# Moving the second weight block's preparation from the first tick to the sixth

## The chip, the cores and the metric

The kernel is one program on one core of a Trainium2 chip. The core has five instruction streams that run side by side and meet through semaphores: TensorE (PE, with its weight loads shown as PEld), VectorE (DVE), ScalarE (ACT), GpSimd (POOL) and SyncE (SP). SP, ACT and POOL also issue DMAs; the profile names their issuing side SPq, ACTq and POOLq. The metric is the device time of one execution in microseconds (us), lower being better.

## The reference

The inputs are float64. Attention over 8 batches, 8 heads, 576 positions and 64 columns a head is followed by a gated feed-forward layer with 512 columns in and 1536 in the middle:

```python
scores = scale * np.matmul(q, k.transpose(0, 1, 3, 2))
s_pos = np.maximum(s, 0.0)
cum = np.cumsum(s_pos, axis=-1)
bias = -(cum[:, :, :, None] - cum[:, :, None, :])
scores = np.where(causal, -1000000000.0, scores + np.minimum(bias, 0.0))
attn = softmax(scores)                       # max, exp, sum, division by hand
x = np.matmul(attn, v)                       # heads side by side: 4608 x 512
gate = 1.0 / (1.0 + np.exp(-(x @ w_gate)))
out = (gate * (x @ w_val)) @ w_out
```

The bias of a row of scores is a constant of the row plus the running sum of its column, so a head needs one row of 576 numbers, which is copied to all 128 partitions.

## The kernel before

**Ticks.** The main loop (L900) runs over ticks `n`. A head has five tiles of rows (`TILES`, `NTL` = 5), so tick `n` belongs to head `i = n // 5`, and the first head is ticks 0 to 4. Its work is spread over several ticks: scores at tick `n`, subtraction of the minimum and the exponential one tick later, turning and the product with v after that. The first eight heads (`NN` = 8) are computed in float32 by functions whose names begin with `n_`; the later ones with operands split into 16-bit pairs. The feed-forward layer starts at tick 44 (`NE`) and runs beside the attention from then on.

**One early head.** `n_prep` turns q and k on PE (L614) and copies them out of PSUM on ACT (L618, L619, L621). `n_s` multiplies them (L631). `n_max` adds the bias row and finds the row's minimum on DVE (L643, with a short read of the accumulator), and then ACT takes the exponential (L644). `n_turn` transposes the exponentials on PE (L653) and copies them out on ACT (L654). `n_av` multiplies with v (L662). The tiles of a head come from the widest, t = 4 (576 columns), to the narrowest, t = 0 (64 columns); the exponential of (0, 0) is the last of the first head and is traced in tick 5.

**The bias rows.** The running sums of all heads are made at the start on DVE (L162 to L166) and stored to DRAM (L167). Each head after the first loads its row back on SP (`load_crow`, L447), and POOL copies it to all partitions (`spread_crow`, L451). DVE's L643 of that head needs it.

**The weight blocks.** The weights are 18 blocks: 12 of w_gate and w_val, 6 of w_out. `load_weight(n)` issues the two DMAs of a block, 512 KB each: on SP for blocks 0 and 1 (L284, before the loop), on ACT for the others (L286, and L279 for w_out). `weight_step` (L365) takes the next block: it first issues the loads whose room has come free, then `decode_weight` turns the pairs of 32-bit words of a float64 into float32 (L298 on ACT, L299 to L301 on DVE), and `split_weight` finds a scale for the block (eight matmuls L310, then DVE L313, L332, L334) and splits it in two 16-bit parts (L337 on ACT, L338 on DVE). Three rooms serve the first 12 blocks in turn (`room`): block 3 takes block 0's, block 4 takes block 1's. So the step of block 1 issues the loads of blocks 2 and 3, and the step of block 2 that of block 4. In the profile the first room is `ws` (decoded into `wa`), the two others lie in `w2all`.

**When steps come.** Before tick 44 the loop traces steps by L1044, up to `min(2 + n // 8, 6)`: blocks 0 and 1 in tick 0, block 2 in tick 8, block 3 in tick 16. The squares of v (L186, fed by POOL's loads L184) come in ticks 1 to 4.

**What sets the order.** A planner that simulates the program orders each engine's instructions (L1125): of those that it takes to be ready it picks by priority, which follows the order of tracing, except that the first heads' work is raised by `first()`. Each engine then runs its list strictly in that order. Two tools bend it: `keep_in_program_order` puts an instruction behind the one traced just before it on its engine (the loads of block 2 have it, L288), and `issue_after(x)` puts all that is traced inside it on the engine of `x` behind `x`; both are about the order of issue and add no wait for an end.

Of the kernel before, what the change touches and what calls it, by code (L numbers as in the profile page):

```python
# [14 lines left out]
AF = mybir.ActivationFunctionType  # L15
# [10 lines left out]
def tile_attention_then_gated_ffn(  # L26
# [11 lines left out]
    nc = tc.nc  # L38
# [11 lines left out]
    NTL = len(TILES)  # L50
# [32 lines left out]
    def halves(x):  # L83
        return x.rearrange("p (a n) -> p a n", a=2)
# [11 lines left out]
    e_t, pf_t = {}, {}  # L96
# [156 lines left out]
    def room(n):  # L253

        o, f = wsteps[n]
        if o == 0:
            return raw[f % 3], dec[f % 3], n - 3
        i, j, last = outroom[f // 2]
        return raw[i], dec[j], last

    def load_weight(n):
        o, f = wsteps[n]
        fs = slice(f * P, (f + 1) * P)
        r, d, _ = room(n)
        for x, src in enumerate((w_out,) if o else (w_gate, w_val)):
            src = src[f * P : (f + 2) * P, :] if o else src[:, fs]
            if wide:
                src = src.bitcast(I32)
                dst = r.rearrange("p n t -> p (n t)")
            else:  # L270
                dst = d.bitcast(F32)
            if o == 0:
                src = src.rearrange("(c p) n -> p c n", p=P)
                dst = dst.rearrange("p (c x n) -> p c x n", c=NC, x=2)[:, :, x]
            else:

                src = src.rearrange("(x p) (h n) -> x p h n", p=P, h=8)
                dst = dst.rearrange("p (h x n) -> x p h n", x=2, h=8)
                ins = nc.scalar.dma_start(dst[0], src[0])  # L279
                if n < NF + 2:  # L280
                    tc.keep_in_program_order(ins)
                src, dst = src[1], dst[1]
            if n < 2:
                nc.sync.dma_start(dst, src)  # L284
            else:
                ins = nc.scalar.dma_start(dst, src)  # L286
                if n == 2 or NF <= n < NF + 2:
                    tc.keep_in_program_order(ins)  # L288

    def decode_weight(n):  # L290

        o, f = wsteps[n]
        r, a, _ = room(n)
        if not wide:
            return a.bitcast(F32), None
        m = w2all[:, f // 2].rearrange("p l h x n -> p (l h x n)") if o else w1[f].rearrange("p c g l n -> p (c g l n)")
        m = m.bitcast(I32)
        nc.scalar.activation(a.bitcast(F32), r[:, :, 1].bitcast(F32), AF.Copy, scale=2.0 ** -112)  # L298
        nc.vector.tensor_scalar(m, a, 3, 0x7FFFFFF8, ALU.logical_shift_left, ALU.bitwise_and)  # L299
        nc.vector.scalar_tensor_tensor(a, a, -0x80000000, m, ALU.bitwise_and, ALU.bitwise_or)  # L300
        nc.vector.scalar_tensor_tensor(a, r[:, :, 0], 29, a, ALU.logical_shift_right, ALU.bitwise_or)  # L301
        return a.bitcast(F32), m
# [60 lines left out]
    wnext = {"load": 0, "step": 0, "tick": 0}  # L363

    def weight_step():  # L365
        n = wnext["step"]
        while n and wnext["load"] < len(wsteps) and room(wnext["load"])[2] < n:
            if not NF <= wnext["load"] < NF + 2:
                load_weight(wnext["load"])
            wnext["load"] += 1  # L370
        split_weight(n, *decode_weight(n))
        wnext["step"] = n + 1
# [213 lines left out]
                                    x16.rearrange("p l n -> p (l n)"))  # L586


    qT, kT, nA = {}, {}, {}

    def n_load(p):
        b, h0 = divmod(2 * p, H)
# [42 lines left out]
    def n_max(i, t):  # L635
        q0, m, w = TILES[t]
        acc = wp.tile([P, 1], F32, tag="em", name=f"em{i}_{t}", bufs=3)[:m]
        ps, r, e = scores_of(i, t), rl[i][:m, :w], e_t[t][:m, :w]
        if w > 512:
            ps, r, e = ps[:m, :, : w // 2], halves(r), halves(e)  # L640
        else:
            ps = ps[:m, :w]
        nc.vector.tensor_tensor_reduce(e, ps, r, 1.0, MASKED, ALU.add, ALU.min, acc)  # L643
        nc.scalar.activation(e_t[t][:m, :w], e_t[t][:m, :w], AF.Exp, bias=acc, scale=-1.0)  # L644

    def n_turn(i, t):

# [245 lines left out]
    NE, NOFF = 44, 87  # L893
# [6 lines left out]
    for n in range(nticks + 12):  # L900
        if n == NTL * EARLY:
            more_room()
        i, t = divmod(n, NTL)
# [41 lines left out]
        if i < NH:  # L945
            p, j = divmod(i, 2)
            b, h = divmod(i, H)
            if t == 0 and i + 1 < NH:
                load_crow(i + 1)
            if t == (2 if i >= NN else 0) and i + 1 < NH:  # L950
                spread_crow(i + 1)
            if i + 2 < NN:
                if j == 0 and t == 1:
                    n_load(p + 1)
                    load_v(p + 1)
                if j == 1 and t == 2:
                    with first():
                        n_prep(p + 1)
            elif j == 0 and i + 2 < NH:
                if t == (2 if spare else 1 if i >= NN else 0) and p + 1 not in qk32:  # L960
                    load_qk(p + 1)
                if t == 2 and i < NN:
                    load_v(p + 1)
            if NN <= i and i + 1 < NH and j == 1 and t == 2:
                load_v(p + 1)
            if NN <= i and j == 0 and t == 0:
                split_v(p)
            if not spare:
                late = i >= NN
                if i + 2 >= NN and j == 0:  # L970
                    if t == 2 + late:
                        qk_square(p + 1)
                    if t == 3 + late:
                        qk_scale(p + 1)
                if n == NTL * (NN - 1) - 1 or NN <= i and t == 0:
                    split_qk(max(i + 1, NN))
                if n == NTL * (NN - 1) + 1 or NN <= i and t == 2:
                    swap_k(i + 1)
            elif i <= EARLY + 1:
                if j == 0:  # L980
                    if t == 1:
                        split_qk(i + 1)
                    if t == 3:
                        swap_k(i + 1)
                        load_qk(p + 2)
                else:
                    if t == 0:
                        qk_square(p + 1)
                    if t == 1:
                        qk_scale(p + 1)  # L990
                    if t == 2:
                        split_qk(i + 1)
                    if t == 4:
                        swap_k(i + 1)
                        split_qk(i + 2)
                        load_qk(p + 3)
            elif j == 0 and i + 2 < NH:
                if t == 0:
                    if i == EARLY + 2:
                        swap_k(i + 1)  # L1000
                    qk_square(p + 1)
                if t == 1:
                    qk_scale(p + 1)
                if t == 2:
                    split_qk(i + 2)
                if t == 4:
                    swap_k(i + 2)
            elif j == 1 and i + 2 < NH:
                if t == 1:
                    split_qk(i + 2)  # L1010
                if t == 3:
                    swap_k(i + 2)
                    if i + 6 < NH:
                        load_qk(p + 3)
            if b == 0:
                if 1 <= n < 1 + vch:
                    v_square(0, n - 1)
                if n == 1 + vch:
                    v_scale(0)
            if b == 0:  # L1020
                if t == 2 and 1 <= h < 1 + vch:
                    v_square(1, h - 1)
                if t == 4 and 1 <= h < 1 + vch:
                    v_square_sum(1, h - 1)
                if t == 1 and h == 6:
                    v_scale(1)
            elif b == 1:
                if VSQ <= n < VSQ + vch:
                    v_square(2, n - VSQ)
                if VSQ + 5 <= n < VSQ + 5 + vch:  # L1030
                    c = VSQ + 4 + vch - n
                    v_square_sum(2, c)
                if n == VSQ + 11:
                    v_scale(2)
            elif b + 1 < B:
                if t == 0 and 2 <= h < 2 + vch:
                    v_square(b + 1, h - 2)
                if t == 4 and 2 <= h < 2 + vch:
                    v_square_sum(b + 1, h - 2)
                if t == 4 and h == 2 + vch:  # L1040
                    v_scale(b + 1)
            if n in OUT:
                load_weight(NF + OUT.index(n))
            while n < NE and wnext["step"] < min(2 + n // 8, 6):  # L1044
                weight_step()

        if n >= NE and state["u"] < 2 * NF:
            fdone = min(NF, int((n - NE + 1) * FPT))
# [19 lines left out]
        m = n - (11 if n > 2 * NTL * H + 30 else 7)  # L1068
# [60 lines left out]
```

## Time and profile before

| what | value |
|---|---|
| median of 3 runs | 1143.78 us |
| lowest and highest run | 1140.69, 1146.30 us |
| the profiled execution, its own time | 1143.07 us |
| its span, first to last instruction | 1141.3 us |
| mean granted TensorE clock | 0.99 |
| PE busy | 1091.1 us, 96% of the span |
| DVE busy | 829.2 us, 73% |
| ACT busy | 753.0 us, 66% |
| POOL busy | 201.2 us, 18% |
| read from and written to HBM, mean | 58 GB/s over the span |

The shares are means over stages with different limits: what a change in the first 30 us is worth has to be read from those 30 us and from whether what follows can keep a gain. A row of the timeline gives start, duration, engine, line, operation, tiles, and in brackets how long the engine stood idle before it and what ended that. A row of the chain of waits gives start, duration and what the end of the program was waiting for at that time. A row of the table by stretches gives, for each engine, its busy time and count, then the granted TensorE clock, the share of the DMA engines and GB/s.

### The profile page before, as it was taken

The numbers are of one execution on the slowest core, as the hardware profiler recorded it, in microseconds if no ns is written. First come the engines' busy times: TensorE is split into PE (matmuls) and PEld (weight loads), VectorE is DVE, ScalarE is ACT, GpSimd is POOL, SyncE is SP. The second block draws the span as 40 slices with busy tenths as digits, with TensorE's granted clock in tenths as the row PEclk, the third lists the DMA queues.
The fourth block names the chain that finished last, engine by engine and source line by source line (L and its number), as shares of the span: only waits on it lengthen the run. The fifth ranks groups of instructions, "written<-read, shape, count | busy, mean of one in ns | idle before, by whom it ended". The sixth has DMA issues, their size and how long they took to land.

```text
span 1141.3 us, 30312 instructions
## 1 busy us (share of the span) xinstructions
PE 1091.1 (96%) x11796; PEld 854.8 (75%) x11796; DVE 829.2 (73%) x2357; ACT 753.0 (66%) x1474; POOL 201.2 (18%) x471
## 2 busy tenths in 40 slices
PE   6897878899999999999999999999999999999998
PEld 4776766757787787788777777778877887787775
DVE  6758989876787777766565577777777779682854
ACT  5868667767786777676656577768776666343533
POOL 3302101022232222221111112212121212000000
PEclk9999889999999999999999999999999999999999
DMA  9776896997989798775736469787977664200000
GB/s 270 215 206 140 180 165 144 183 186 163 174 176 173 158 177 162 155 152 116 169 66 149 103 152 164 150 166 156 179 134 164 145 117 93 41 20 2 20 1 37
DMA packets 445357, 157.62 MB, mean 138 GB/s; under 512 B 403551, under 2 KB 435295, under 8 KB 445214
## 3 DMA queue, kind: packets, MB, share of 16 engines
q1 hardware_dynamic: 418974, 128.17, 57.6%
q10 hardware_dynamic: 23040, 16.78, 5.0%
q0 software_dynamic: 3200, 10.75, 2.6%
q8 instruction: 92, 1.51, 0.5%
q14 instruction: 51, 0.42, 0.1%
HBM read 56.92 MB, written 9.58 MB: 58 GB/s over the span
## 4 chain that ended last, share of the span: by engine, by line
PE 70%; DMA 9%; DVE 8%; issue 5%; ACT 4%; SPq 2%; POOL 1%; ACTq 0%; POOLq 0%; DVEq 0%
PE gv L714 33%; PE o L745 21%; PE tv L831 3%; PE s L491 3%; PE s L489 2%; DMA v<-in_v_dram 2%; PE ta L831 1%; DVE e L529 1%; PE av L564 1%; PE av L562 1%; PE av L563 1%; PE na_ps L662 1%; DMA T<-qk 1%; DMA w2all<-in_moe_w_out_dram 1%; DMA x<-x 1%
## 5 line engine op out<-in xcount | busy, mean ns | idle before, releaser
L714 PE MATMUL gv<-x,w 128*128 128x256 f16 (+3 forms) x6336 | 553.9, 245 | 9.8 <-DVE t2f L721 8.8
L714 PEld LDWEIGHTS <-w 128*128 128x128 f16 x6336 | 480.2, 98 | 63.4 <-issue 12.0
L745 PE MATMUL o<-w2all,h 128*128 128x512 f16 x1296 | 313.9, 379 | 1.9 <-ACT h L729 1.9
L530 ACT ACTIVATE e<-e,em 128x576 f32<-128x576 f32 x280 | 153.1, 556 | 88.8 <-DVE em L529 86.0
L745 PEld LDWEIGHTS <-h 128*128 128x128 f16 x1296 | 123.4, 98 | 109.1 <-ACT h L729 2.3
L511 POOL TENSOR_SCALAR_AFFINE_SELECT rl<-rl 128x128 f32<-128x128 f32 (+1 forms) x240 | 88.4, 369 | 499.2 <-DVE em L529 456.2
L529 DVE CUSTOM_DVE_ANT_0 e<-s,rl,qkcf 128x576 f32<-128x576 f32 x280 | 151.2, 544 | 28.8 <-PE s L491 12.8
L729 ACT ACTIVATE h<-t,hsc 128x256 f16<-128x256 f32 x192 | 96.3, 503 | 92.7 <-DVE t L721 90.4
L719 ACT ACTIVATE th<-gv,scb 128x256 f32<-128x256 f32 (+3 forms) x264 | 99.0, 403 | 65.5 <-PE gv L714 53.9
L539 DVE SCALAR_TENSOR_TENSOR p<-e,p 128x384 f16<-128x384 f32 x224 | 103.2, 499 | 41.1 <-ACT p L534 40.3
L721 DVE SCALAR_TENSOR_TENSOR t<-th,gv 128x256 f32<-128x256 f32 x168 | 69.7, 415 | 63.9 <-ACT th L719 63.8
L534 ACT ACTIVATE p<-e 128x1152 f16<-128x1152 f32 x112 | 111.9, 1000 | 3.4 <-DMA pt<-p 0.9
L730 DVE SCALAR_TENSOR_TENSOR h<-t,hsc,h 128x256 f16<-128x256 f32 x192 | 93.4, 487 | 27.4 <-ACT h L729 25.0
L562 PE MATMUL av<-v,pt 128*128 128x65 f16 x560 | 67.7, 193 | 2.5 <-DMA pt<-p 2.5
L451 POOL PARTITION_BROADCAST cr<-cr x63 | 59.4, 949 | 55.9 <-ACT th L719 21.1
L489 PE MATMUL s<-T 128*128 128x288 f16 (+2 forms) x246 | 64.5, 280 | 3.8 <-DVE em L529 3.0
L563 PE MATMUL av<-v,pt 128*128 128x64 f16 x560 | 67.7, 192 | 0.0
L564 PE MATMUL av<-v,pt 128*128 128x65 f16 x560 | 67.6, 194 | 0.0
L491 PE MATMUL s<-T 128*128 128x288 f16 (+2 forms) x246 | 61.5, 277 | 4.0 <-DMA T<-T 4.0
L562 PEld LDWEIGHTS <-pt 128*128 128x128 f16 x560 | 52.5, 98 | 8.3 <-DMA pt<-p 3.4
L563 PEld LDWEIGHTS <-pt 128*128 128x128 f16 x560 | 52.5, 97 | 4.5
L564 PEld LDWEIGHTS <-pt 128*128 128x128 f16 x560 | 52.7, 97 | 0.2
(209 smaller groups left out, 1539.9 us busy)
## 6 DMA issues: line engine op xcount, KB each, us to landing
v<-v SPq DMA_DIRECT2D x56, 162.5 KB
v<-in_v_dram SPq DMA_DIRECT2D x64, 128.0 KB
out_dram<-io POOLq DMA_DIRECT2D x32, 256.0 KB, 3.4
T<-T SPq DMA_DIRECT2D x82, 72.0 KB
t2f<-in_v_dram SPq DMA_DIRECT2D x20, 288.0 KB
qk<-in_q_dram SPq DMA_DIRECT2D x17, 288.0 KB
qk<-in_k_dram SPq DMA_DIRECT2D x17, 288.0 KB
w2all<-in_moe_w_gate_dram ACTq DMA_DIRECT2D x7, 512.0 KB
```

Of the source, the lines that this page charges most:

```text
L491: nc.tensor.matmul(ps[:, : b_ - a], lhs, T[i][:, 2, a:b_], start=False, stop=not mask)
L529: nc.vector.tensor_tensor_reduce(e, ps, r, c, MASKED, ALU.add, ALU.min, acc)
L530: nc.scalar.activation(e_t[t][:, :w], e_t[t][:, :w], AF.Exp, bias=acc, scale=-1.0)
L534: nc.scalar.activation(p_s[h_][:, 0], e_s[h_], AF.Copy, scale=PSCALE)
L539: nc.vector.scalar_tensor_tensor(flat[:, LOW[t] * P : (LOW[t] + t) * P], e_t[t][:, : t * P], PSCALE, flat[:, kb * P : (kb + t) * P], ALU.m ...
L562: nc.tensor.matmul(AV[i][:, t], hi, v_[:, D : 2 * D + 1], start=kb == 0, stop=False)
L563: nc.tensor.matmul(AV[i][:, t, 0:D], hi, v_[:, 0:D], start=False, stop=False)
L564: nc.tensor.matmul(AV[i][:, t], lo, v_[:, D : 2 * D + 1], start=False, stop=False)
L714: nc.tensor.matmul(ps[:, gv, a:e], w1[f][:, cc, gv, wl], x_of(b, cc)[:, xl, c0 + a : c0 + e], start=(c == 0), stop=(c == 3 * NC - 1))
L719: nc.scalar.activation(th[:, a:e], ps[:, 0, a:e], AF.Tanh, scale=scb[b][:, f : f + 1])
L729: nc.scalar.activation(h[:, 0], t2, AF.Copy, scale=hsc[:, f : f + 1])
L745: mm = nc.tensor.matmul(ps[:m], h[:, hl, tt * P : tt * P + m], w2[f][:, wl], start=(f == 0 and c == 0), stop=(f == NF - 1 and c == 2))
```

## The change

`n_max` keeps the exponential of the first head's last tile in a list. The loop traces only one weight step in ticks 0 to 4, so the second block's step is traced in tick 5, after that exponential, and everything that this step puts on ACT (the DMA issues of blocks 2 and 3, L298 and L337) is queued behind it. The number of steps from tick 5 on is as before.

```diff
-    qT, kT, nA = {}, {}, {}
+    qT, kT, nA, e_last = {}, {}, {}, []
...
         nc.vector.tensor_tensor_reduce(e, ps, r, 1.0, MASKED, ALU.add, ALU.min, acc)
-        nc.scalar.activation(e_t[t][:m, :w], e_t[t][:m, :w], AF.Exp, bias=acc, scale=-1.0)
+        ins = nc.scalar.activation(e_t[t][:m, :w], e_t[t][:m, :w], AF.Exp, bias=acc, scale=-1.0)
+        if (i, t) == (0, 0):
+            e_last.append(ins)
...
-            while n < NE and wnext["step"] < min(2 + n // 8, 6):
-                weight_step()
+            while n < NE and wnext["step"] < min((1 if n < NTL else 2) + n // 8, 6):
+                with tc.issue_after(e_last[0].ins) if wnext["step"] == 1 else ExitStack():
+                    weight_step()
```

The loads of block 2 are also kept behind what was traced just before them on ACT: that was L337 of block 0, and is now the exponential itself.

## The prediction

> **What bounds the kernel now.** First the table by stretches, cut at 250 and 260 us, to see which stage can keep a gain.
>
> ```profile
> 0.00:260.00 260.00, 218.16 (x1951) 171.05 (x1952) 209.83 (x594) 190.12 (x355) 45.08 (x96) 0.96 0.82 188
> 250.00:1141.30 891.30, 882.89 (x9906) 688.99 (x9904) 625.33 (x1779) 569.22 (x1131) 158.10 (x380) 1.00 0.62 124
> ```
>
> The first busy time is PE's. From 250 us on it is busy 882.89 of 891.30 us, so only 8.41 us are idle: a gain that arrives there reaches the end nearly whole. In the first 260 us it is idle 41.84 us and no engine is full: there chains of waits decide, and the change lies in that part. The chain that ended last shows which:
>
> ```profile
> 8.20 7.67 DMA w2all<-in_moe_w_val_dram
> ...
> 15.89 1.12 ACT w2all L298
> 17.01 0.56 ACT e L644
> ```
>
> The end of the program hangs on the second half of block 1's load (issued at 8.20, landed at 15.87), then on ACT's decoding of that block, then on an exponential of the first head. A weight block that nothing needs yet holds up attention. The timeline shows why:
>
> ```profile
> 14.11 0.08 DVE L643 DVE_READ_ACCUMULATOR2_ANT em<- 128x1 f32 x1
> 15.66 0.08 DVE L643 DVE_READ_ACCUMULATOR2_ANT em<- 128x1 f32 x1
> 15.94 0.08 DVE L643 DVE_READ_ACCUMULATOR2_ANT em<- 128x1 f32 x1
> 15.89 1.12 ACT L298 ACTIVATE w2all<-w2all 128x1024 f32<-128x1024 f32 x1 [3.56 <-DMA w2all<-in_moe_w_val_dram]
> 16.15 0.08 DVE L313 DVE_READ_ACCUMULATOR wj<-wps 128x1 f32 x1
> 16.91 0.66 ACT L644 ACTIVATE e<-e,em 128x448 f32<-128x448 f32 x1
> 17.05 0.69 DVE L299 TENSOR_SCALAR w<-w2all 128x1024 int32<-128x1024 int32 x1 [0.82 <-ACT w2all L298]
> 17.66 0.21 DVE L643 CUSTOM_DVE_ANT_0 e<-s,cr 64x64 f32<-64x64 f32 x1
> 20.03 0.35 ACT L644 ACTIVATE e<-e,em 64x64 f32<-64x64 f32 x1
> ```
>
> The minimum of tile 3 (448 columns) was ready at 14.19, yet its exponential began at 16.91: ACT stood 3.56 us before L298. DVE likewise waited with L299 in front of the minimum of the last tile.
>
> **The change part by part.** *Head 0.* With L298 behind the last exponential, the one of tile 3 can begin at 14.19, 2.72 us earlier; tiles 2 and 1 are ready at 15.74 and 16.02. DVE is free for the last tile's minimum at 16.23, so that is done at about 16.5. With 0.56 and 0.47 us for the exponentials of tiles 2 and 1 (estimated from the 0.66 and 0.35 us of the rows beside them) and perhaps one 0.5 us copy between, the last exponential ends at 17.0 to 17.5 instead of 20.38.
>
> *Step 1 on its engines.* It adds no instruction. L298 (1.12 us) begins at 17.0 to 17.5, 1.1 to 1.6 us later than now. Whether that costs anything is seen at the end of its DVE part, where the room comes free for block 4:
>
> ```profile
> 17.86 1.21 DVE L300 SCALAR_TENSOR_TENSOR w2all<-w2all,w 128x1024 int32<-128x1024 int32 x1
> 21.34 0.29 DVE L313 TENSOR_SCALAR_CACHE_REDUCE wj<-wps 128x128 bf16<-128x128 f32 x1 [2.21 <-PE wps L310]
> 21.55 1.22 DVE L301 SCALAR_TENSOR_TENSOR w2all<-w2all 128x1024 int32<-128x1024 int32 x1
> 23.20 0.37 ACTq L286 DMA_DIRECT2D w2all<-in_moe_w_gate_dram  x1
> ```
>
> L299, L300 and L301 take 0.69 + 1.21 + 1.22 = 3.12 us, after L298 from 18.1 to 18.6: they can be over at 21.2 to 21.7, where they now end at 22.77, because DVE today lies idle 2.21 us inside the step. Block 4's load (23.20) comes no later. I put this at nothing; the cover is that idle time, and if the planner leaves it where it is, L301 ends at about 24, 1.2 us late.
>
> *The four DMA issues* of blocks 2 and 3 move too, past what ACT has queued:
>
> ```profile
> 17.62 0.44 ACTq L286 DMA_DIRECT2D ws<-in_moe_w_gate_dram  x1
> 18.68 0.39 ACTq L286 DMA_DIRECT2D ws<-in_moe_w_val_dram  x1
> 19.63 0.38 ACTq L286 DMA_DIRECT2D w2all<-in_moe_w_gate_dram  x1
> 20.12 0.45 ACTq L286 DMA_DIRECT2D w2all<-in_moe_w_val_dram  x1
> 29.36 1.13 ACT L298 ACTIVATE wa<-ws 128x1024 f32<-128x1024 f32 x1
> ```
>
> From 17.0 on, back to back (1.66 us), they begin at a mean of 17.6 to 18.1 instead of 19.0: some 1.2 us earlier, not later. Block 3 is wanted at 29.36 and ACT does not wait there, so nothing is gained by it.
>
> *Where the gain is cut.* Head 1 needs its bias row first:
>
> ```profile
> 19.00 0.84 SPq L447 DMA_DIRECT2D cr<-cum_d  x2
> 23.52 1.24 POOL L451 PARTITION_BROADCAST cr<-cr  x1 [4.07 <-DMA cr<-cum_d]
> 24.79 0.76 DVE L643 CUSTOM_DVE_ANT_0 e<-s,cr 128x576 f32<-128x576 f32 x1 [0.69 <-POOL cr L451]
> 25.47 0.08 DVE L643 DVE_READ_ACCUMULATOR2_ANT em<- 128x1 f32 x1
> 25.07 1.15 ACT L337 ACTIVATE w<-w2all,wscale 128x1024 f16<-128x1024 f32 x1
> 27.69 0.41 ACT L619 ACTIVATE nq<-nq_ps 64x288 f32<-64x288 f32 x1
> 28.12 1.33 ACT L644 ACTIVATE e<-e,em 128x576 f32<-128x576 f32 x2
> ```
>
> The row lands at about 23.5 whatever head 0 does, POOL's copy and DVE's minimum follow, and 25.55 is the earliest start of head 1's first exponential. It begins at 28.12 now, since ACT is still at head 0's leftovers, L337 of block 1 and head 2's q and k. So the gain at head 1 is at most 28.12 - 25.55 = **2.57 us**, though head 0 itself gains 2.9 to 3.4. L337 goes ahead into time in which ACT is idle today; one copy such as L619 (0.41) will probably still stand in the way. Bounds: 0 (the copies and squares fill the place) and 2.57; I take 2.57 - 0.41 = 2.16, about **2.2 us**, near the upper end, because the large item (1.15) moves and the small ones are what is left.
>
> *What is carried to 250 us.* What comes next are ACT and DVE chains whose order moves along; the loads of blocks 2 and 3 are early by then. I take all of it. Sum: 1143.07 - 2.2 = 1140.9 us for the profiled execution; that lay 0.71 us under the median of 1143.78, so on the medians' scale **1141.6 us**.
>
> **The rivals.** *The DMA engines give it back.* Between 19 and 24 us the queues stand so, in the answer on DMAs (packets, MB, share of 16 engines; q10 carries ACT's loads, q1 SP's):
>
> ```profile
> q10 hardware_dynamic: 1052, 1.05, 68.3%
> q1 hardware_dynamic: 731, 0.18, 16.2%
> ```
>
> The engines are full, and SP's bias row of 2.2 KB needs from 19.00 to 23.5. Loads that begin 1.2 us earlier take, at that share, 0.683 x 1.2 = 0.8 us of them away from SP's queue before the row has landed. Then 25.55 becomes 26.35 and the gain 2.2 - 0.8 = 1.4 us: 1142.4; if a square's load on POOL also moves ahead, none is left: 1143.8. For it: the share of the engines is over 80% for the two queues together. Against: the 1.2 us count only as far as SP's queue is not empty. [...]
>
> *More is gained than head 1.* PE idles in front of the stall and is then granted a lower clock:
>
> ```profile
> 14.00:16.00 2.00, 0.47 (x3) 0.32 (x3) 2.00 (x8) 0.11 (x1) 0.57 (x1) 1.00 1.03 214
> 16.00:18.00 2.00, 0.38 (x2) 0.38 (x3) 1.18 (x9) 2.00 (x4) 0.00 (x0) 0.74 0.91 217
> 18.00:20.00 2.00, 2.00 (x9) 1.71 (x8) 1.14 (x2) 2.00 (x6) 0.54 (x1) 0.50 0.93 196
> 32.00:34.00 2.00, 0.93 (x9) 0.69 (x8) 1.71 (x2) 2.00 (x8) 0.91 (x2) 1.00 1.01 227
> 34.00:36.00 2.00, 2.00 (x11) 1.88 (x11) 0.87 (x2) 2.00 (x4) 0.50 (x1) 0.50 0.93 238
> 36.00:38.00 2.00, 2.00 (x8) 1.11 (x7) 1.05 (x1) 0.51 (x1) 0.00 (x0) 0.64 0.85 274
> 33.42 0.44 PE L662 MATMUL na_ps<-v,p 128*128 128x65 f32 x2 [1.07 <-ACT p L654]
> ```
>
> After 14 to 18 us, with PE busy 0.85 of 4 us, the clock is 0.50. The same comes again after 32 us, and there it lies on head 2's scores: at full clock 34 to 38 would be 2 x 0.50 + 2 x 0.36 = 1.7 us shorter. If an ACT that is less behind takes away the wait of 1.07 and that drop, and head 1 gains its 2.57, the sum is 5.3; a further 1.1 us saved out of the 41.84 idle by the new plan makes 6.4: 1137.4. Against: each of them must come, and further idle time may appear as easily as go. [...]
>
> *It is slower: the planner keeps head 0 late and step 1 goes into head 1.* If copies and squares of ACT are planned ahead of the last exponential, so that it still ends at 20.38, then L298 ends at 21.5 and the 3.12 us on DVE at 24.6; block 0's L338, today at 22.76, comes after:
>
> ```profile
> 22.76 1.28 DVE L338 SCALAR_TENSOR_TENSOR w<-wa,wscale,w 128x1024 f16<-128x1024 f32 x1
> ```
>
> Then head 1's minimum waits until 24.6 + 1.28 = 25.9 instead of 24.79 (1.1 us), and block 4's room is free 1.8 us later. With both on the path: 1143.78 + 2.9 = 1146.7. It decides when L301 of block 1 ends behind 22.77; when L338 of block 1 (1.28) and block 3's decoding also fall in front of minima, 1.28 + 1.12 + 3.12 = 5.5 more, up to 1152. For it: the planner put L298 in front of exponentials before, so its picture of landings is off. Against: the tiles of the first heads are raised in priority, and the squares are not.
>
> *The change does nothing:* the exponential of tile 3 waits for another load, such as that of a square of v. That is the 1143.8 end of the first rival.
>
> **How the numbers follow.** Forecast (1140.3 to 1142.8 as its own range): 0.50. DMA engines or nothing, 1142.4 to 1143.8: 0.20. More gained, around 1137.4: 0.18. Slower, around 1146.7: 0.12. A measurement of this kernel tells 0.5% (5.7 us) from no change, so faster means under 1138.1 and slower over 1149.5. Most of the gain rival and a tail of the forecast, for a plan that differs further on, give 0.19 faster; the far part of the slower rival and the same tail 0.09; 0.72 within. The range leaves out half of each outer rival and some tail: 1135.5 to 1147.
>
> **What would show it.** Right: the chain no longer passes through block 1's load; tile 3's exponential begins by 14.5, the last ends by 17.6; L298 of block 1 comes then, L301 ends by 22; the bias row still lands at about 23.5 and head 1's first exponential begins at 25.6 to 26.1; no 0.50 clock at 18 to 20; 1.5 to 2.6 us gained at 60 us and at 250 us. Wrong: the row lands after 24.3 (DMA engines), the last exponential ends at 20 (slower), or the gain at 36 us is not the gain at 250 us: then the carrying is the wrong step.

## The result: 1.05% slower

| | before | after |
|---|---|---|
| median (4 runs each) | 1142.78 us | 1156.98 us |
| lowest and highest run | 1140.69, 1146.30 us | 1153.49, 1158.44 us |
| the profiled execution | 1143.07 us | 1158.44 us |
| its span | 1141.3 us | 1156.7 us |

The ratio is 1.0105, with a 95% interval of 1.0084 to 1.0127. The forecast was 1141.6 us, in a range from 1135.5 to 1147.

First the place that the change is about. The timeline of the changed kernel, ACT, DVE and POOL between 10 and 30 us (start, duration, engine, line, tiles; in brackets the idle time before and what ended it):

```profile
14.66 0.67 ACT L644 ACTIVATE e<-e,em 128x448 f32<-128x448 f32 x1 [1.90 <-DVE em L643]
17.45 0.70 ACT L644 ACTIVATE e<-e,em 128x192 f32<-128x192 f32 x2
18.57 1.15 ACT L337 ACTIVATE w<-wa,wscale 128x1024 f16<-128x1024 f32 x1 [0.42 <-issue]
20.37 1.17 ACT L298 ACTIVATE w2all<-w2all 128x1024 f32<-128x1024 f32 x1 [0.66 <-ACT w L337]
22.13 2.52 POOL L451 PARTITION_BROADCAST cr<-cr  x2 [4.93 <-DMA cr<-cum_d]
25.27 1.22 DVE L301 SCALAR_TENSOR_TENSOR w2all<-w2all 128x1024 int32<-128x1024 int32 x1
24.63 0.78 ACT L644 ACTIVATE e<-e,em 128x576 f32<-128x576 f32 x1 [0.17 <-DVE em L643]
```

Tile 3's exponential begins at 14.66 (before 16.91), head 0's last one ends at 18.15 (before 20.38), and head 1's first begins at 24.63 (before 28.12). So the wait that was to go is gone, and head 1 begins 3.5 us sooner in this pair of profiles (how far one order scatters is told with the second experiment).

Now the same table by stretches that the prediction opened with, for the changed kernel:

```profile
0.00:260.00 260.00, 212.84 (x1836) 168.64 (x1837) 203.25 (x573) 182.57 (x340) 46.40 (x90) 0.91 0.79 180
250.00:1156.70 906.70, 898.79 (x10033) 698.75 (x10031) 637.34 (x1813) 581.23 (x1156) 163.37 (x387) 1.00 0.61 125
```

From 250 us on PE is idle for 7.91 us (before 8.41): that part is as full as it was. The loss lies in the first 260 us, where PE does less work (212.84 us busy, before 218.16) and does it at a lower mean clock (0.91, before 0.96). Cut finer, first before, then after:

```profile
0.00:40.00 40.00, 27.92 (x173) 21.41 (x174) 27.45 (x63) 25.12 (x49) 13.32 (x39) 0.91 0.91 262
40.00:60.00 20.00, 18.11 (x149) 15.49 (x146) 15.55 (x47) 16.99 (x39) 6.09 (x11) 1.00 0.73 222
60.00:120.00 60.00, 51.29 (x403) 41.84 (x402) 44.28 (x142) 49.60 (x94) 8.54 (x14) 0.97 0.67 157
120.00:140.00 20.00, 17.02 (x211) 14.46 (x209) 20.00 (x49) 10.85 (x17) 2.98 (x4) 0.91 0.97 208
140.00:200.00 60.00, 49.00 (x520) 40.85 (x517) 54.39 (x147) 44.13 (x73) 5.11 (x7) 0.94 0.78 154
200.00:240.00 40.00, 36.26 (x380) 26.93 (x381) 34.85 (x116) 27.96 (x55) 4.51 (x13) 1.00 0.93 182
240.00:340.00 100.00, 96.14 (x1148) 71.78 (x1147) 73.95 (x224) 76.36 (x157) 25.78 (x57) 1.00 0.88 174
```
```profile
0.00:40.00 40.00, 31.09 (x210) 23.93 (x210) 29.04 (x75) 27.21 (x57) 16.29 (x44) 1.00 0.92 270
40.00:60.00 20.00, 17.18 (x100) 13.91 (x99) 13.55 (x30) 14.33 (x30) 6.23 (x5) 0.79 0.76 221
60.00:120.00 60.00, 50.21 (x390) 41.09 (x389) 42.47 (x135) 47.45 (x88) 8.02 (x14) 0.93 0.61 145
120.00:140.00 20.00, 13.03 (x107) 9.78 (x108) 18.80 (x48) 10.99 (x18) 2.42 (x2) 0.67 0.90 188
140.00:200.00 60.00, 51.72 (x582) 44.25 (x581) 50.57 (x134) 40.72 (x67) 5.23 (x8) 0.94 0.73 155
200.00:240.00 40.00, 29.62 (x288) 22.84 (x286) 32.57 (x105) 28.75 (x58) 2.85 (x6) 0.95 0.84 150
240.00:340.00 100.00, 97.07 (x1111) 71.11 (x1110) 70.47 (x201) 68.64 (x143) 22.44 (x50) 0.97 0.88 164
```

One number makes such rows comparable. The end of this kernel is a long stretch in which PE is nearly always busy (898.79 of the 906.70 us from 250 us on), so what counts is how much PE work is done when that stretch begins. A stretch of length T with PE busy for b at a mean granted clock c has **lost** T - b x c: in 40 to 60 us that is 20 - 18.11 x 1.00 = 1.9 before and 20 - 17.18 x 0.79 = 6.4 after. That PE's work goes with the granted clock is the author's estimate, from 18 products with v that took 3.94 us at 0.50 and 2.12 us at 1.00 (rows below). By stretch:

| lost PE time, us | 0-40 | 40-60 | 60-120 | 120-140 | 140-200 | 200-240 | 240-340 | sum |
|---|---|---|---|---|---|---|---|---|
| before | 14.6 | 1.9 | 10.2 | 4.5 | 13.9 | 3.7 | 3.9 | 52.7 |
| after | 8.9 | 6.4 | 13.3 | 11.3 | 11.4 | 11.9 | 5.8 | 69.0 |

The sums differ by 16.3 us, the spans by 15.4. The reader is to see two things. In the first 40 us the change gains 5.7 us, more than forecast (in these two profiles). By 60 us 4.5 of them are gone, and then 120 to 140 and 200 to 240 us lose some 7 and 8 us more, in work that the change doesn't name.

### The profile page after: what moved, and what is told of

Same layout as the page of the kernel before. It is cut to its first block, busy times and chain, and to the rows that moved or that the text cites. A ratio compares the mean times of both kernels' runs of the same rounds, so it can differ in the third digit from the quotient of the medians.

```text
span 1156.7 us, 30319 instructions
## 1 busy us (share of the span) xinstructions
PE 1101.6 (95%) x11796; PEld 862.1 (75%) x11796; DVE 831.5 (72%) x2357; ACT 754.5 (65%) x1474; POOL 206.6 (18%) x471
## 4 chain that ended last, share of the span: by engine, by line
PE 76%; DMA 7%; DVE 6%; ACT 5%; issue 3%; SPq 1%; POOL 1%; ACTq 0%; POOLq 0%; DVEq 0%
PE gv L716 38%; PE o L747 22%; PE s L489 3%; PE s L491 3%; PE tv L833 3%; DMA T<-qk 2%; PE ta L833 1%; PE av L564 1%; PE av L562 1%; PE av L563 1%; DMA v<-in_v_dram 1%; DMA pt<-p 1%; DVE e L529 1%; ACT e L644 1%; PE tu L833 1%
## 5 line engine op out<-in xcount | busy, mean ns | idle before, releaser
L732 DVE SCALAR_TENSOR_TENSOR h<-t,hsc,h 128x256 f16<-128x256 f32 x192 | 93.5, 487 | 27.3 <-ACT h L731 24.9
L451 POOL PARTITION_BROADCAST cr<-cr x63 | 63.2, 1008 | 79.9 <-DMA cr<-cum_d 79.8
L562 PE MATMUL av<-v,pt 128*128 128x65 f16 x560 | 69.1, 194 | 8.0 <-DMA pt<-p 8.0
L564 PE MATMUL av<-v,pt 128*128 128x65 f16 x560 | 69.1, 196 | 0.0
```

The lines of the kernel that those rows point to most:

```text
L562: nc.tensor.matmul(AV[i][:, t], hi, v_[:, D : 2 * D + 1], start=kb == 0, stop=False)
L564: nc.tensor.matmul(AV[i][:, t], lo, v_[:, D : 2 * D + 1], start=False, stop=False)
```

## The experiments

Two questions: why isn't the early gain carried, and where do the further 15 us come from? Four theories, by their letters in the expectations. **M** (or L): block 1 is now late, and that costs. **C**: TensorE drops to half clock (granted 0.50) in the new order. **N**: the planner's new order behind the first heads is worse. **P**: any change of the trace gives a new order, good or bad by chance.

To tell them apart the order was taken out of the planner's hands. The program is traced once for each plan, the 16401 instructions are numbered alike in both, and then each engine gets a list by edges that order issue without adding a wait (code here and below is shortened):

```diff
+    for order in lists_by_engine:
+        for x, y in zip(order, order[1:]):
+            tc.add_manual_dep(y, x.name, NoSync)
```

So one kernel can have one plan up to the first minimum of some head and the other plan behind it. All runs in one table; each ratio is to before in the same session, and the lost PE time is worked out by the formula above from the rows of the one profiled execution. Three profiles of before's order (before, e2, e3) have sums of 52.7 to 55.4 us, so differences of that size mean nothing:

| kernel | median us (runs) | ratio, 95% | 0-40 | 40-60 | 60-140 | 140-340 | sum |
|---|---|---|---|---|---|---|---|
| before | 1142.8 to 1145.6 | 1 | 14.6 | 1.9 | 14.7 | 21.5 | 52.7 |
| after | 1156.98 (4) | 1.0105, 1.0084 to 1.0127 | 8.9 | 6.4 | 24.6 | 29.1 | 69.0 |
| e1 two moved | 1145.76 (12) | 1.0019, 1.0001 to 1.0036 | 17.6 | 2.4 | 14.6 | 21.8 | 56.4 |
| e2 before's order | 1144.86 (10) | 1.0008, 0.9991 to 1.0025 | 13.6 | 3.7 | 16.1 | 22.0 | 55.4 |
| e3 before's order | 1145.23 (10) | 1.0010, 0.9995 to 1.0024 | 12.0 | 3.5 | 15.5 | 21.8 | 52.8 |
| e4 sixth tick only | 1146.78 (10) | 1.0031, 1.0011 to 1.0050 | 10.9 | 2.6 | 15.3 | 23.8 | 52.7 |
| e5 after to head 4, before | 1159.79 (4) | 1.0117, 1.0088 to 1.0146 | 9.0 | 6.9 | 22.4 | 23.8 | 62.1 |
| e6 after to head 9, before | 1148.95 (10) | 1.0028, 1.0008 to 1.0049 | 9.2 | 6.6 | 16.5 | 24.9 | 57.0 |
| e7 before to head 4, after | 1155.20 (4) | 1.0091, 1.0060 to 1.0122 | 13.1 | 1.9 | 22.4 | 26.5 | 63.8 |
| e8 before to head 9, after | 1155.17 (4) | 1.0079, 1.0048 to 1.0111 | 13.3 | 1.9 | 25.2 | 24.7 | 65.1 |
| e9 after, fillers | 1156.33 (5) | 1.0097, 1.0062 to 1.0132 | 9.8 | 2.1 | 22.7 | 26.6 | 61.2 |
| e10 after, before in 9 to 12 | 1158.20 (4) | 1.0112, 1.0089 to 1.0134 | 11.7 | 6.0 | 16.1 | 36.7 | 70.6 |
| e11 after, before in 14 to 21 | 1153.34 (9) | 1.0079, 1.0054 to 1.0104 | 10.9 | 5.5 | 22.4 | 19.2 | 58.0 |
| e12 as e6, fillers | 1147.30 (11) | 1.0016, 0.9993 to 1.0039 | 8.9 | 2.1 | 17.6 | 25.0 | 53.6 |
| e13 step in the fourth tick | 1153.11 (5) | 1.0087, 1.0056 to 1.0118 | 12.9 | 2.4 | 15.8 | 30.7 | 61.9 |
| e14 other anchor | 1148.10 (10) | 1.0026, 1.0007 to 1.0046 | 7.8 | 4.2 | 16.7 | 27.3 | 56.0 |
| e15 SP's order alone | 1166.73 (4) | 1.0190, 1.0160 to 1.0219 | 13.7 | 1.9 | 19.5 | 39.9 | 75.0 |
| e16 all but SP's | 1193.46 (4) | 1.0401, 1.0348 to 1.0454 | 12.6 | 1.9 | 26.6 | 55.0 | 96.1 |
| e17 e4 to head 12, before | 1146.12 (12) | 1.0018, 0.9997 to 1.0039 | 10.8 | 2.6 | 21.0 | 23.8 | 58.3 |
| e18 e14 to head 11, before | 1140.92 (12) | 0.9978, 0.9960 to 0.9995 | 8.7 | 6.0 | 13.9 | 22.8 | 51.3 |

(In e9 and e12 up to 2.7 us of PE's busy time are the fillers' own, so their lost time is up to that much higher. One of e16's four runs took 2895 us; nothing in the records explains it.)

**The move by itself.** Before's order is pinned; only L298 of block 1 goes behind head 0's last exponential, and L299 behind that tile's minimum:

```diff
+    for what, behind in ((l298, exps[4]), (l299, minima[4])):
+        plan.remove(what)
+        plan.insert(plan.index(behind) + 1, what)
```

> Every engine keeps the order that the planner gave it before the change; only two instructions are moved: ACT's L298 of block 1 behind the first head's last exponential, DVE's L299 of block 1 behind that tile's minimum. Nothing is planned anew. Theory N (the step moved as predicted gains; the loss comes from the new order that the planner gives to all that follows): head 1's first minimum as before (24.8 us), its first exponential 1 to 2.5 us earlier than 28.1, 1 to 3 us gained at head 2 and at the end, so 0.997 to 0.999 of before. Theory M (a late block 1 is itself what costs, through its room, its loads or the work that it pushes into head 1): slower, 1.005 or more.

Measured: 1.0019. Neither branch came: no gain, and less than half of the loss that M asks for. Head 1's first minimum came 2.2 us later than before (27.0). The timelines of ACT and DVE in this run say why:

```profile
14.05 0.67 ACT L644 ACTIVATE e<-e,em 128x448 f32<-128x448 f32 x1 [1.63 <-DVE em L643]
18.37 0.45 ACTq L286 DMA_DIRECT2D ws<-in_moe_w_gate_dram  x1
18.87 0.56 ACT L644 ACTIVATE e<-e,em 128x320 f32<-128x320 f32 x1 [2.63 <-DMA nqk<-in_q_dram]
20.89 1.09 ACT L298 ACTIVATE w2all<-w2all 128x1024 f32<-128x1024 f32 x1
24.07 1.15 ACT L337 ACTIVATE w<-wa,wscale 128x1024 f16<-128x1024 f32 x1 [2.08 <-DVE wscale L334]
25.36 1.68 DVE L338 SCALAR_TENSOR_TENSOR w<-wa,wscale,w 128x1024 f16<-128x1024 f32 x1
27.02 0.74 DVE L643 CUSTOM_DVE_ANT_0 e<-s,cr 128x576 f32<-128x576 f32 x1
```

Tile 3's exponential is early (14.05), but the issue of block 3's first load (18.37; `ws` is block 3's room) still stands in ACT's list ahead of tile 2's exponential, which waits there for 2.63 us. The bracket of that row names a load of q as what ended the wait. The stall has only changed its name. On DVE block 1's pieces and then block 0's L338 stand in front of head 1's minimum. So these two moves gain nothing; the issues of the loads, which the change moves too, stayed where they were, and the whole step moved with all else pinned was not run. For M the run is a measure: block 1's L298 is 5.0 us later than before (20.89, before 15.89), and that costs 0.2%, not 1%.

**Two more measurements of before.** These two kernels, as built, have before's order on every engine, instruction for instruction, so their expectations were not tested; they show how one order scatters.

> All that the planner before puts ahead of head 4's first minimum is given in the order of the changed kernel, all the rest in the order of before. In the changed kernel head 4 begins 0.7 us later than before. Theory N: the rest is the old order, so the time is that of before within 2 us (0.998 to 1.002). Theory M: what is late early stays late, so most of the 14 us is there (1.008 or more).

> The mirror image: up to head 4's first minimum the order of before, from there on the order of the changed kernel. Theory N: 12 to 16 us slower than before (1.010 to 1.014), without block 1 being moved at all. Theory M: the time of before (0.998 to 1.003).

Measured: 1144.86 us (ratio 1.0008, 0.9991 to 1.0025) and 1145.23 us (1.0010, 0.9995 to 1.0024). In their profiles head 2's first minimum begins at 37.0 and 36.1, where it began at 38.1 in the profile of before: 2 us of scatter for one and the same order.

The scatter reaches the reading on which the change rests. Four more runs below (e7, e8, e15, e16) have before's order up to 60 us at least. In the profiles of these six, ACT waits 1.16 to 2.08 us in front of L298 of block 1 (before: 3.56), tile 3's exponential begins 0.3 to 1.3 us behind its minimum (before: 2.72), and the chain of waits doesn't pass through block 1's load. The stall that the prediction read was the longest of seven. In the first 40 us the seven profiles of before's order lose 12.0 to 14.6 us, the seven of the changed kernel's order (after, e5, e6, e9 to e12) 8.9 to 11.7: on the mean 13.3 and 9.8. The early gain of the order is thus some 3.5 us, not 5.7. Head 1's first exponential begins at 26.6 to 28.1 in the ones and at 24.6 to 26.2 in the others, with medians of 27.4 and 25.4.

**The tick without the rule on ACT.** `issue_after` is left out:

```diff
-                with tc.issue_after(e_last[0].ins) if wnext["step"] == 1 else ExitStack():
-                    weight_step()
+                weight_step()
```

> The step is traced in the sixth tick, without the tie to the exponential; the planner then still puts L298 of block 1 ahead of the exponential of tile 3, as before, but plans the rest anew. The stall in the first head stays (L298 at 15.9, the exponential of tile 3 at 16.9). Theory N: any time from 0.995 to 1.015, as the new order falls out; a difference of over 3 us with the first 25 us unchanged speaks for it. Theory M: the time of before (0.998 to 1.002), as block 1 comes when it came.

Measured: 1.0031. L298 of block 1 stands ahead of tile 3's exponential again (14.59, after a wait of 2.24 us for its load), and yet head 2 begins 4.9 us earlier than in the profile of before (33.2), 2.9 us earlier than in the earliest profile of before's order (36.1). So that lead doesn't need the stall to go; it belongs to the new order. By 340 us it is lost (52.7 us of PE time lost by then in both).

**Where in the order.** Four splices of the two plans:

```diff
+    order = [i for i in first_plan if i in upto_head] + [i for i in other_plan if i not in upto_head]
```

> Every engine keeps the changed kernel's order (block 1's part late) for what stood ahead of head 4's first minimum in the kernel before, and the order of before for the rest. In the changed kernel's trace heads 2 and 3 began 5.5 us sooner than before and head 4 was 0.7 us late. Theory N (the loss is made by the new order behind head 4): this keeps a lead of 2 to 6 us at head 2 and gives 1138 to 1143 us. Theory M (block 1's later scale and split make the loss, in whatever order the rest stands): 1150 to 1157 us. Theory C (the loss is a half clock that the early order brings on at 52 us, 10 us long, and that comes again later by itself): head 4 late, and 1146 to 1157 us.

> The same with the seam at head 9's first minimum. In the changed kernel's trace head 9 was 3.9 us late and the lasting 15.5 us were complete only by 315 us. Theory N: no more than some 4 us lost, 1143 to 1148 us. Theory M and theory C: 1150 to 1157 us.

> The reverse of the first: the order of before, with block 1's part early, up to head 4's first minimum, and the changed kernel's order of everything behind it. Theory N: the loss is in the order behind the seam, 1153 to 1160 us, without any later block. Theory M and theory C: nothing is lost, 1141 to 1146 us.

> The same with the seam at head 9's first minimum. Theory N: the 11 us or so that the changed kernel's trace loses between head 9 and head 22 are lost here too, 1150 to 1156 us. Theory M and theory C: 1141 to 1146 us.

Measured: 1.0117, 1.0028, 1.0091, 1.0079 (1159.8, 1149.0, 1155.2 and 1155.2 us: the last two as theory N has it, the second between the branches, the first outside all of them). The last two take M out for the larger part: with block 1 early as before, the changed kernel's order behind head 9 alone costs 0.8% (9 us). The second is its counterpart: the early order costs 0.3% (3 us); block 1 is late in it, so here M is not excluded. Together they make the 12 us by which the changed kernel is slower. That is theory N for the 9 us. The first doesn't fit it: a seam at head 4 costs more than the whole plan, with a further half-clock stretch soon behind the seam (70.2 us, 6.8 us long; mean clock 0.74 from 60 to 80 us). Plans can't be cut anywhere.

**Half clock at 51.6 us.** The changed kernel's rows, cut at the bounds of the clock's stretches:

```profile
48.19:51.60 3.41, 1.82 (x11) 1.11 (x12) 3.41 (x6) 3.35 (x9) 2.01 (x1) 1.00 0.00 1
51.60:55.01 3.41, 2.80 (x13) 1.96 (x11) 3.05 (x5) 2.83 (x8) 1.37 (x1) 0.50 0.84 266
55.01:58.43 3.42, 3.42 (x17) 3.28 (x16) 0.43 (x2) 0.00 (x0) 0.00 (x0) 0.50 1.21 306
58.43:61.84 3.41, 3.41 (x11) 2.37 (x11) 0.00 (x0) 0.00 (x0) 0.00 (x0) 0.50 0.68 215
```

After 3.4 us in which PE was busy for only 1.82, the clock is 0.50 for three such stretches. DVE and ACT are all but idle in the last two: both wait for PE's scores of head 4, which stand behind 18 products with v. The rows of the timeline, for PE, DVE and ACT:

```profile
55.37 3.94 PE L664 MATMUL na_ps<-v,p 128*128 128x65 f32 x18
62.23 0.76 DVE L643 CUSTOM_DVE_ANT_0 e<-s,cr 128x576 f32<-128x576 f32 x1 [6.79 <-PE s L518]
63.03 1.34 ACT L644 ACTIVATE e<-e,em 128x576 f32<-128x576 f32 x2 [8.58 <-DVE em L643]
```

PE had been waiting there for copies by ACT (2.0 us for L656 between 40 and 60 us), which had two L298 between them (44.78 and 48.95). The test is to give PE something to do in those waits, 17 transposes of the identity into PSUM columns that nothing reads:

```diff
+    def more(ps, real, *which):
+        for _ in range(FILL.get(which, 0)):
+            fill.append((real, nc.tensor.transpose(ps[:, 3 * P :], ident, ident).ins))
```

> The changed kernel's order on every engine, and in front of 51 us seventeen more transposes of the identity on TensorE, into PSUM columns that nothing reads, in places where it waited for copies (about 2.5 us of work at full clock). In the changed kernel TensorE was busy 0.53 of the 3.4 us before 51.6, and its clock was then 0.50 for 10.2 us, in which DVE waited 6.8 us for head 4's scores. Theory C for this place (the low share brings the half clock, and the half clock the wait): no half clock between 48 and 62, head 4 begins at 57.5 to 59 where it began at 62.2, and TensorE time lost (idle time and half of the busy time at half clock) by 60 us is 11 to 13 where it was 15.6. The whole: 1152 to 1154 us if that lead is kept, 1155 to 1158 if the waits behind take it. Theory N (the order alone, whatever the clock): head 4 at 61 to 63.

> The changed kernel's order to head 9, before's order behind it (1148.95 us in an earlier run), and the same seventeen transposes in front of 51 us. Theory C at 51 us and theory N behind head 9 together: no half clock between 48 and 64, head 4 at 57.5 to 59, and 1143 to 1145 us, if a lead of some 4 us is carried as far as a delay of 4 us was in the run that moved two instructions. If it is given back: 1147 to 1150 us.

The same places in the run with the changed kernel's order and fillers:

```profile
48.02:51.43 3.41, 2.19 (x17) 1.68 (x18) 3.41 (x9) 3.36 (x8) 1.28 (x1) 1.00 0.00 1
54.84:58.26 3.42, 3.42 (x26) 3.11 (x26) 1.19 (x2) 0.23 (x1) 0.00 (x0) 1.00 1.21 319
55.25 2.12 PE L670 MATMUL na_ps<-v,p 128*128 128x65 f32 x18
58.98 0.76 DVE L648 CUSTOM_DVE_ANT_0 e<-s,cr 128x576 f32<-128x576 f32 x1 [2.95 <-PE s L518]
```

No half clock in the first 60 us (mean clock 1.00 from 0 to 40 and from 40 to 60 us); the 18 products take 2.12 instead of 3.94 us, DVE waits 2.95 instead of 6.79, and head 4 begins at 58.98 instead of 62.23. So C is shown for this place: with PE busy for 2.19 of 3.41 us in place of 1.82 ahead of it, the half clock stays away, and the wait is shorter. It is no accident of one execution: all five profiles of this order without fillers (after, e5, e6, e10, e11) have a half clock of 10.2 to 13.7 us that begins between 49 and 55 us, and neither of the two with fillers has one there (mean clock from 40 to 60 us 0.74 to 0.85 in the five, 1.00 in the two). But the whole is 1.0097, where the changed kernel has 1.0105: the 3 us do not reach the end, as the second branch of the expectation had it. With before's order behind head 9 the fillers bring 1.0028 to 1.0016, within the intervals no difference.

**Places further on.** The chain of waits at head 10 reads so, first in before, then in after (start, duration, what the end of the program was waiting for):

```profile
119.18 0.60 DVE qk L429
119.78 0.53 DVE qk L431
```
```profile
125.15 1.22 DVE wa L301
126.36 0.53 DVE qk L431
126.89 0.54 DVE w L299
127.43 7.79 DMA T<-qk
```

In the changed kernel's order, DVE scales head 10's q and k behind more pieces of weight blocks, and is done 6.6 us later (126.9, before 120.3). The transpose that brings them to PE is issued only 3.5 us later (127.43, before 123.97), since SP is held by transposes of p in both (8.37 us from 118.08, before 4.53 us from 119.33); it then takes 7.79 us, where before PE began the scores 4.3 us after the issue. Two repairs put before's order in place of the changed kernel's, between heads 9 and 12 and between heads 14 and 21:

> The changed kernel's order, but before's order for what stands between head 9's and head 12's first minimum in the kernel before. In the changed kernel's trace TensorE lost 11.6 us between 120 and 140 (before 4.7), in front of the transposes of head 10's q and k, whose scaling on DVE came behind three more pieces of weight blocks. Theory N (the order at this place): 4 to 6 us lost there, 1148 to 1152 us. If the loss comes from what arrives late from further ahead: 10 to 12 us lost there, 1155 to 1158 us.

> The changed kernel's order, but before's order between head 14's and head 21's first minimum. The changed kernel lost 18 us of TensorE time between 200 and 320 us (before 7.6). Theory N: 8 to 10 us lost there, 1146 to 1150 us. If the loss comes from further ahead: 1154 to 1158 us.

Each repair works where it is made. Between 120 and 140 us the first loses 4.0 us (after 11.3); between 200 and 240 us the second loses 3.4 us (after 11.9, before 3.7). But the first loses it again: 18.0 us between 140 and 200 (after 11.4), and ends at 1.0112, like the changed kernel. Its time, 1158.2 us, is about that of the other branch, although the place itself was repaired. The second is at 1.0079 (1153.3 us), between its two branches. What a place seems to cost in the trace is not what its repair is worth.

**Which queue.** Behind head 9, SP's list alone from the changed kernel's plan, then all lists but SP's:

> Before's program and order, with only SyncE's queue (the issues of loads and transposes) in the changed kernel's order behind head 9. The run with all engines so gave 1155 us. Theory S (the order of the issues on SyncE makes the loss behind head 9): 1150 to 1156 us. Theory K (the order on DVE, ScalarE and TensorE, where pieces of weight blocks stand ahead of head 10's q and k, makes it): 1143 to 1147 us.

> The reverse: behind head 9 TensorE, DVE, ScalarE and GpSimd take the changed kernel's order, SyncE keeps before's. Theory S: 1143 to 1147 us. Theory K: 1150 to 1157 us.

Measured: 1.0190 and 1.0401, against 1.0079 for all lists together. Both theories fail: neither list is bad by itself. Half a plan is worse than either whole one. The author's reading, which no run shows to be the cause, is that SP then holds transposes in an order in which the engines don't make their inputs: between 100 and 340 us SP waits in front of L550 for DVE's p (L547) for 29.8 and 42.0 us (before 22.7, after 29.7), and PE waits for transposes of p (L550, issued on SP) for 11.1 and 18.5 us in these two, 7.9 in e8 and 2.5 in before.

The same wait separates the two orders behind head 9. It is 1.7 to 2.9 us in the nine profiles that have before's order there (before, e1, e2, e3, e5, e6, e12, and from head 12 and 11 on e17 and e18) and 6.0 to 8.1 in the four that have the changed kernel's (after, e7, e8, e9). That points to these transposes for a good part of the 9 us, but doesn't prove it: in e10 the wait is 3.4 us, and the kernel is as slow as after.

**Other changes of the same step.** The step in the fourth tick, without a rule on ACT; and the change as it is, but behind the exponential of head 0's third tile (parts of the lines):

```diff
-min((1 if n < NTL else 2) + n // 8, 6)
+min((1 if n < 3 else 2) + n // 8, 6)
```
```diff
-        if (i, t) == (0, 0):
+        if (i, t) == (0, 2):
```

> Block 1's step is issued in the fourth tick, with no rule about ScalarE: a third order of the same 16401 instructions, which differs from before's and from the changed kernel's on TensorE in over 1400 places. Theory P (every new trace gives a new order behind head 4, and these orders differ among themselves by some 10 us, whatever was moved): anywhere from 1140 to 1158 us, and not near the run that had the sixth tick alone. Theory L (what costs is that block 1 comes late): between before's 1145 and the changed kernel's 1157, in order of the tick: 1146 to 1148 us.

> The change, but ScalarE's part of block 1 stands behind the exponential of head 0's third tile in place of the last. ScalarE's part comes some 2 us sooner than in the changed kernel. Theory L: 1150 to 1157 us, near the changed kernel. Theory P: the place of the anchor foretells nothing, 1140 to 1158 us, and the stretches where TensorE loses time are others than 51, 120 and 220 us.

Measured: 1.0087 and 1.0026. L foretold the reverse (near before, and near after). P fits, as far as such a wide range can: the second loses most between 60 and 120 us (13.5) and between 140 and 200 us (17.7), though it too is granted less than the full clock between 40 and 60 us (0.91). In order of how late block 1 comes (fourth tick, sixth tick, behind the third tile, behind the last) the ratios are 1.0087, 1.0031, 1.0026, 1.0105: no order in it. Five plans of the same instructions span 1.1%, and before's is the fastest of them.

**An early lead in front of before's order.**

> The order that the sixth tick alone gave, up to head 12's first minimum in the kernel before, and before's order behind it. In its own run the sixth tick alone was 2.5 us ahead of before in TensorE time lost by 140 us (29.7 against 32.2) and level by 200 us. Theory O (a lead is lost to a worse order behind it; before's order would carry it): 1140 to 1143 us. Theory W (before's order behind head 9 has waits of its own that an early start does not move): 1144 to 1147 us.

> The order that the rule behind head 0's third tile gave, up to head 11's first minimum in the kernel before, and before's order behind it. That order had the largest lead of all, 7.1 us at head 8 and 3.0 us of TensorE time lost by 140 us. Theory O: 1140 to 1143 us. Theory W: 1144 to 1147 us.

Measured: 1.0018 and **0.9978 (0.9960 to 0.9995)**: the first as theory W has it, the second as theory O. The second is faster than before and after: a gain of 0.2% that its interval barely tells from none, and the best of seventeen other kernels tried, so it may be chance. Against the profile of before it leads by 6.3 us at head 2, keeps 2.7 through a half clock at 51.7 us (mean clock 0.83 from 40 to 60 us), and is 3.6 ahead at head 24; so a lead can be carried. The first had 5.0 us at head 2 and 3.2 at head 5, and lost them in one step. Its rows, and the same place in the run of the sixth tick alone, which has the same order there:

```profile
72.60:76.07 3.47, 1.71 (x18) 1.41 (x17) 0.86 (x7) 1.85 (x6) 0.00 (x0) 1.00 0.89 246
76.07:79.48 3.41, 3.41 (x18) 3.34 (x17) 1.28 (x1) 1.31 (x3) 0.00 (x0) 0.51 1.18 284
79.48:82.90 3.42, 3.42 (x14) 2.94 (x14) 0.72 (x3) 2.00 (x2) 0.00 (x0) 0.50 0.62 147
82.90:86.30 3.40, 3.40 (x11) 2.13 (x10) 2.50 (x7) 2.27 (x4) 0.20 (x1) 0.50 0.00 1
```
```profile
72.06:75.47 3.41, 1.85 (x22) 1.59 (x20) 1.20 (x8) 1.96 (x6) 0.03 (x1) 1.00 0.94 262
75.47:78.89 3.42, 3.40 (x26) 3.19 (x27) 1.28 (x1) 1.73 (x4) 0.00 (x0) 1.00 1.10 294
```

PE was busy for 1.71 of 3.47 us in the one and 1.85 of 3.41 in the other. The one was granted half clock for 10.2 us and went from 3.2 us ahead to 1.0 behind; the other kept the full clock (1.00). The busy share alone doesn't decide it: in before, 1.99 of 3.41 us brought a half clock at 34.0 us (rows in the last section).

## Why the prediction was wrong

*The wait that goes* was read rightly from the profile, but it was the longest of seven: six other profiles of before's order have 1.16 to 2.08 us in front of L298 where 3.56 was read, and no chain through block 1's load. In the changed kernel the chain no longer passes through block 1's load, tile 3's exponential begins at 14.66 (14.5 forecast), and there is no half clock at 18 to 20 (mean clock 1.00 over the first 40 us, before 0.91).

*Head 0* ends at 18.15 where 17.0 to 17.5 was forecast: three copies and a square stand between its exponentials, not one copy.

*Step 1 on its engines*: L298 begins at 20.37, behind block 0's L337, and L301 ends at 26.5 instead of by 22, since DVE takes head 1's first minima before it. That is 3.7 us later than before; the case costed at "about 24, 1.2 us late" was too small.

*The four issues* come at 18.08, 18.59, 19.20 and 19.80: on the mean 0.1 us earlier than before, not 1.2. The rival built on those 1.2 us had no ground.

*The cap at head 1* was not as firm as it was put. The bias row was taken to land at 23.5 whatever head 0 does; POOL took it up at 22.13, and at 21.5 to 23.4 in the six other profiles of before's order. In the pair of profiles head 1's exponential gained 3.5 us; by the medians of seven profiles each it is 2.1, close to the forecast of 2.2, though by another way than L298 alone (e1, e4). The first 40 us lost 8.9 us instead of 14.6: 5.7, close to the 5.3 of the rival that saw more gained; on the mean of the profiles it is 3.5.

*The step that failed* is "What is carried to 250 us": "What comes next are ACT and DVE chains whose order moves along [...] I take all of it." The order didn't move along; it was made anew on every engine. The runs showed in its place: (1) the first gain is at least in part the new order's, since two instructions moved with all else pinned gain nothing (e1), and the new order leads with the stall still there (e4); (2) in the changed kernel that lead is spent at 51.6 us on a half clock (0.50 for 10.2 us) that the new order brings on (e9), for this place shown by taking it away; (3) behind head 9 the new order loses 9 us, with block 1 early too (e8); (4) other changes of the same step give other orders and other times, up to 1.1% apart (e4, e13, e14).

*The rival on the slow side* had the wrong mechanism. It saw step 1 fall into head 1's minima, at most 1152 us. In the changed kernel DVE's minimum of head 1 came early (23.84), and the loss arose 30 to 300 us later; in e1, where step 1 did fall in front of that minimum, the end lost 2 us. The prediction's own "the planner put L298 in front of exponentials before, so its picture of landings is off" was the right ground for a rival that stands in it only as "a tail of the forecast, for a plan that differs further on", without a price: that a new plan is a new draw, while the old one, by the five seen here, was a good one.

What stays open: what in the order behind head 9 makes its 9 us (PE's longer wait for transposes of p points to SP, without proof), since the queues can't be exchanged one by one (e15, e16) and repaired places lose again (e10); what the whole step, moved with all else pinned, would bring; and why the planner comes to such different orders.

## What to carry to other kernels

Before pricing a stall, read it in several profiles of the same kernel: here it was 3.56 us in one and 1.16 to 2.08 in six others. Where a planner orders the work, moving one step redraws the order of all that follows: pin the old order and move the step alone before believing a gain worked out locally, and allow for a change of either sign (here 1.1% between the plans) on top of it. Count a lead only as far as the next place where the clock or another engine sets the pace (here 51.6 us), and compare two plans by lost PE time, stretch by stretch, up to where PE is full. A part of a good order can be put in front of another (e18), but every seam has to be measured (e5).

## What was not expected of the hardware

In before a granted clock of 0.50 lasted for one stretch of 3.41 us at 34.0 us, with PE busy for all of it, and the next row is at 1.00. In after, from 51.6 us on, it lasted for three (10.2 us), with PE busy for 2.80, 3.42 and 3.41 us, and in e17, from 76.1 us on, for three as well, with 3.41, 3.42 and 3.40: one stretch in which PE was busy throughout did not always bring the full clock back. Nor does PE's busy time ahead of it tell the cases apart: 1.71 of 3.47 us in e17, 1.82 of 3.41 in after and 1.99 of 3.41 in before were followed by 0.50, and 1.85 of 3.41 in e4 was not. The rows of before:

```profile
30.61:34.02 3.41, 1.99 (x13) 1.21 (x12) 3.06 (x3) 3.41 (x11) 0.93 (x2) 1.00 0.72 176
34.02:37.43 3.41, 3.41 (x14) 2.68 (x13) 1.92 (x2) 2.49 (x4) 0.48 (x1) 0.50 0.90 256
37.43:40.84 3.41, 3.41 (x36) 3.12 (x34) 2.77 (x6) 2.29 (x5) 0.92 (x2) 1.00 0.50 172
```

One order doesn't give one sequence of clocks: e10 and e11 have the changed kernel's order up to head 9, and in them a half clock of 6.8 us from about 24 us, which the changed kernel didn't have (mean clock over the first 40 us 0.91 in both, after 1.00); head 2 began at 34.9 and 35.2 instead of 32.4.
